# Routed attention and an ELU feed-forward: row sums inverted on 32 partitions by way of transfers, weights converted within attention, one form of the second product for all groups

## The chip, the cores and the metric

The kernel runs on one core of a Trainium2 chip. The engines of the core are TensorE (PE, matrix products; PEld is its weight load), VectorE (DVE), ScalarE (ACT), GpSimd (POOL) and SyncE (SP, which here issues transfers, DMAs). The metric is the device time in microseconds of one execution, as the median of several runs.

## The reference

Attention runs over 4 batches, 8 heads, 768 tokens, head size 64. Each query and each key is assigned to one of 16 centroids of its head, and a query sees only the keys of its own cluster:

```python
    mask = q_assign[:, :, :, None] == k_assign[:, :, None, :]
    scores = scale * np.matmul(q, k.transpose(0, 1, 3, 2))
    scores = np.where(mask, scores, -1000000000.0)
    scores = scores - np.max(scores, axis=-1, keepdims=True)
    attn = np.exp(scores)
    attn = attn / (np.sum(attn, axis=-1, keepdims=True) + 1e-09)
    return np.matmul(attn, v).astype(np.float32)
```

Its output, 3072 tokens of 512 values, goes through `h = x @ w_in` (512 to 2048), an ELU, and `g @ w_out` (2048 to 512). The two weights arrive as 64-bit floats, all else is worked in 32 bits.

## The kernel before

**Attention.** There are 32 blocks: batch, half of the queries (384), pair of heads. `slot(n)` is one step of a software pipeline. PE's work in it, in order: the row sums of block n-2 (`row_sums`, L551, a product with ones that spreads each sum over 64 partitions), the products with V of block n-1 (`values`, L533), in some slots a product with the centroids (`similar`, L424), and the scores of block n (L495, with a mask product at L508). ACT takes the exponentials of block n (L517). DVE adds the probabilities over the keys (`sums_begin` L520, `sums_end` L525 and L526), so that the sums of block n are begun at the end of slot n and ended at the start of slot n+1. The division of block n-2 in slot n works on all 128 partitions: ACT takes the logarithm of the sums, a copy of them, and the exponential of minus the logarithm (`take_sums`, L560 to L562); DVE makes one Newton step (`divide`, L565 and L566) and POOL multiplies the block's output with it (L569).

Also in the slots, on DVE: the cluster assignment (L437 to L450), the transposes of the next batch's raw keys and queries (L652 to L666), and the conversion of the 64-bit weights. On SP, in program order within a slot: `load_v(n + 1)` (L179), `load_k` and `load_q` (L163: a `load_k` is 4 transfers, a `load_q` 16), then the 1 MB pieces of 64-bit weights (`ask`, L297). `load_q` comes in slots 1 and 4 of a batch (2 and 4 of the first), `load_k` twice in slot 0 and once in slots 2 and 3. SP issues in order, and an issue that must wait for an engine or for another transfer holds back what comes after it.

**Conversion.** 16 pieces, eight of `w_in`, eight of `w_out`. A piece is fetched to a place (`places`), then a "begin" (L317, L325, and on ACT L327) and three "join" steps (L337, L341, L347) on DVE. `weigh(n)` doles them out: slot n adds ROOM[n] us to a credit, and a step is taken while the credit covers its COST. Four sums of quarters of `w_out` follow (`weight_sum`, L372 to L378). What is left after attention is done at the `fill()` points of group 0.

**Feed-forward.** 3072 tokens in 6 groups of 512. The first product of a group is four units (`unit`, L735) of seven block products each, by a scheme of the Strassen kind, with the additions on DVE and ACT. In a unit, L788 adds product 5 into bank 2 before the block product `block_product(b2, s4, x22, False)`; the ELU is ACT's exponential (L745), a clamp on POOL (L746) and L749 on DVE. A unit has four `fill()` points. In group 0 POOL also makes the sums of `w_in` (`w_step`, L714 to L718) and sends them to DRAM (`w_far`, L719), and later groups fetch them from there (L711).

The second product has seven units of the same scheme over quarters of `w_out`. In groups 1 to 5 each of them is again seven small products (`second_product`, L919, with DVE's `t_step` L962 to L968 and `g_step` L979), 49 in all, of four 128 by 128 products each. For that 33 tables of sums and quarters of `w_out` are made by `table_steps` (28 steps on DVE, L876 to L883, sent to DRAM by L869), two steps at each `fill()` of group 1, and read back part by part (`fetch`, L914). In group 0, `second_product_plain` makes each unit from eight small products per quarter pair, 56 in all, without tables. `verdict` puts the findings of `findings` into a flag that decides whether a general path must run; it doesn't here.

Of the kernel before, what the change touches and what calls it, by code (L numbers as in the profile page):

```python
# [19 lines left out]
P = 128  # L20
# [41 lines left out]
def main_path(ctx, tc, c, q, k, v, centroids, moe_w_in, moe_w_out, out):  # L62
# [77 lines left out]
    r_of = sums_w[:, 6 * HS : 7 * HS]  # L140
    e_of = sums_w[:, 7 * HS : 8 * HS]
# [109 lines left out]
    r_sum = const.tile([P, len(blocks)], F32, name="r_sum")  # L251
    d_sum = const.tile([P, len(blocks)], F32, name="d_sum")
# [21 lines left out]
    places += [(spare.rearrange("p a n -> p (a n)")[:, : 2 * WC].unsqueeze(1), into + 2)]  # L274
# [78 lines left out]
    def by_chunks(x):  # L353
# [9 lines left out]
        "s2": by_chunks(t_all),  # L363
        "s4": by_chunks(sums_w[:, 1536:3584]),
        "s3": by_chunks(words_w[:, :]),
    }

    def weight_sum(n):
# [13 lines left out]
        [0.0, 1.0, 1.3, 1.4, 1.4, 1.7, 2.6, 2.6]  # L382
        + [2.3, 2.6, 3.0, 3.0, 1.4, 1.7, 2.6, 2.6] * (B - 2)
        + [2.3, 2.6, 4.0, 4.0, 2.6, 2.6, 2.6, 2.6]
    )
    COST = {"begin": 1.4, "join": 1.25, "sum": 2.2}
# [11 lines left out]
    def weigh(n):  # L398
        nonlocal credit, now
        now = n  # L400
        credit = min(credit, 2.5) + ROOM[n]
        begun = False
        while steps and credit >= COST[steps[0][0]]:
            kind, m = steps[0]
            if kind == "join" and begun or kind == "sum":
                return
            if kind == "begin" and asked_in.get(m, n) > n - 2:
                return
            credit -= COST[kind]
            begun = begun or kind == "begin"  # L410
            weigh_step(*steps.pop(0))
# [134 lines left out]
    def take_values(n):  # L546
        nc.scalar.activation(x_of(n), o_bank[:, :HS], Act.Copy, scale=-1.0)
# [11 lines left out]
    def take_sums(n):  # L559
        nc.scalar.activation(r_of, d_bank[:, :HS], Act.Ln)  # L560
        nc.scalar.activation(e_of, d_bank[:, :HS], Act.Copy, accum_out=d_sum[:, n : n + 1])
        nc.scalar.activation(r_of, r_of, Act.Exp, scale=-1.0)  # L562

    def divide(n):
        nc.vector.tensor_tensor(e_of, e_of, r_of, op=Alu.mult)  # L565
        nc.vector.scalar_tensor_tensor(  # L566
            r_of, e_of, -2.0, r_of, op0=Alu.add, op1=Alu.mult, accum_out=r_sum[:, n : n + 1]
        )
        nc.gpsimd.tensor_tensor(x_of(n), x_of(n), r_of, op=Alu.mult)  # L569
# [55 lines left out]
    def slot(n):  # L625
# [16 lines left out]
        if n > 1:  # L642
            divide(n - 2)
# [24 lines left out]
        weigh(n)  # L668

# [91 lines left out]
    def unit(k_, u, after_second=None, fill=None):  # L761
# [20 lines left out]
        if k_ == 1 and u == 3:  # L782
# [15 lines left out]
        if k_ > 0:  # L798
            for t in {2: ("t1",), 3: ("t2", "t3", "t4")}.get(u, ()):
                t_step(0, t)  # L800
# [61 lines left out]
    def table_steps():  # L862
# [9 lines left out]
        for n, a in enumerate(("s3", "s4", "s2", "a11", "a12", "s1", "a22")):  # L872
# [21 lines left out]
    for n in range(len(UNITS)):  # L894
# [9 lines left out]
        for _ in range(1, N // GS)  # L904
# [122 lines left out]
    def second_product_plain(k_, early_on):  # L1027

        for n in range(len(UNITS)):
            _, a, b = UNITS[n]  # L1030
            for q_ in range(4):
                for j in range(2):
                    small_product(
                        banks_of(k_, n)[q_],
                        part_g(b, j, q_ % 2),
                        part_w(a, q_ // 2, j),
                        j == 0,
                        j == 1,
                    )
                if n == 0 and q_ == 0:  # L1040
                    flush_all()
                    early_on()
                elif n == 2 and q_ == 1:
                    verdict()
                take(k_, n, q_)
            taken(k_, n)
            if n < 3:
                g_step(n, 0)
                g_step(n, 1)
            if n == 2:  # L1050
                next_group(k_)

    def second_product(k_, ahead):
# [17 lines left out]
        for n in range(len(UNITS)):  # L1071
            b1, b2, b3, b4 = (x[:, :P] for x in banks_of(k_, n))
            part_product(k_, n, "m6")
            nc.scalar.copy(b3, b2)
            if n > 0:
# [34 lines left out]
    def findings():  # L1110
# [3 lines left out]
        nc.vector.tensor_reduce(peak[:, 0:1], r_sum, axis=Axis.X, op=Alu.add)  # L1114
        nc.vector.tensor_reduce(peak[:, 1:2], d_sum, axis=Axis.X, op=Alu.add)
        nc.vector.tensor_scalar(ok[:, 0:1], peak[:, 0:1], -R_MAX, None, op0=Alu.is_gt)
        nc.vector.tensor_scalar(ok[:, 1:2], peak[:, 1:2], D_MAX, None, op0=Alu.is_lt)
# [13 lines left out]
    for n in range(1, len(blocks)):  # L1131
        slot(n)
        if n == 3 * NB + 1:
            places.append((early[:, 6144:].unsqueeze(1), into + 6))
            ask()
# [8 lines left out]
    row_sums(last_n - 1)  # L1144
    values(last_n)
    sums_end()
    for n in range(2):
        places.append((p_out[:, ts(n, 2048)].unsqueeze(1), len(pieces)))
    ask()
    take_sums(last_n - 1)  # L1150
    divide(last_n - 1)
    take_values(last_n)

    def finish_attention():
        row_sums(last_n)
        take_sums(last_n)
        divide(last_n)
# [9 lines left out]

    def fill_weights():
        flush()
        if steps:  # L1170
            weigh_step(*steps.pop(0))

    def early_on():
        while steps:
            weigh_step(*steps.pop(0))
            flush()

    blanks(0)
    for u in range(4):
        if u == 1:  # L1180
            blanks(1)
        run(unit(0, u, finish_attention if u == 0 else None, fill_weights))
        if u == 1:
            findings()
    second_product_plain(0, early_on)

    table = table_steps()

    def fill_table():
# [274 lines left out]
```

## Time and profile before

| what | value |
| --- | --- |
| median of 3 runs | 915.13 us (914.92 to 915.49) |
| the profiled execution | 915.41 us, span 913.5 us from first to last instruction |
| attention | to 341.4 us |
| group 0, four units | 341.4 to 393.8 us |
| group 0, second product | 393.8 to 444.1 us |
| group 1, four units | 444.1 to 492.5 us |
| group 1, second product | 492.5 to 536.4 us |

The page gives one line for each engine with its busy time, then the span in 40 slices with the busy tenths. A view of windows gives, for each stretch, the busy time and number of instructions of PE, PEld, DVE, ACT and POOL, then the clock granted to PE, the share of the DMA engines and GB/s. In a timeline a line is start, duration, engine, source line, operation, out<-in, shape and count, with idle time of the engine before it and who ended it in brackets. A view of one source line gives minimum, median and maximum of its durations in ns, and for transfers the time from issue to landing.

### The profile page before, as it was taken

To read this page: it belongs to the slowest core of one execution; us is meant where nothing else is said; L and a number is where in the kernel's file an instruction comes from. 1 tells how busy PE (TensorE), PEld (TensorE's weight loads), DVE (VectorE), ACT (ScalarE), POOL (GpSimd) and SP (SyncE) were. 2 spreads that over 40 slices of the span, in tenths; PEclk is the share of its full clock that TensorE was granted. 3 is DMA by queue.
4 is the path that set the end of the run, shared out by engine and by line. 5 is a ranking of instruction groups with operands and counts; after the bars stand their busy time and mean duration, and the time that the engine had idled before them with its cause. 6 is when DMAs were issued, how large, how long until landed. Compare 5 with 4: busy or idle time off the path is not lost.

```text
span 913.5 us, 15842 instructions
## 1 busy us (share of the span) xinstructions
PE 898.5 (98%) x6083; PEld 685.4 (75%) x6083; DVE 673.8 (74%) x980; ACT 416.9 (46%) x819; POOL 201.5 (22%) x197
## 2 busy tenths in 40 slices
PE   7999999999999999999999999999999999999996
PEld 5444444444444448899988998999899989998996
DVE  4799999999999996982389843684369446944584
ACT  5767787777778764410133223322332233223321
POOL 1022121131304326750025002400230013102200
PEclk9999999999999999999999999999999999999999
DMA  6755554354325431110297852185218521762172
GB/s 201 190 107 150 139 137 104 103 110 128 68 83 137 146 110 69 52 42 2 87 319 263 285 170 66 45 280 173 70 37 278 182 69 36 266 196 61 45 224 81
DMA packets 143331, 121.22 MB, mean 133 GB/s; under 512 B 88208, under 2 KB 104592, under 8 KB 142224
## 3 DMA queue, kind: packets, MB, share of 16 engines
q1 hardware_dynamic: 142000, 115.93, 43.2%
q0 software_dynamic: 1248, 4.20, 1.5%
q8 instruction: 50, 0.82, 0.4%
q14 instruction: 33, 0.27, 0.1%
HBM read 100.96 MB, written 18.09 MB: 130 GB/s over the span
## 4 chain that ended last, share of the span: by engine, by line
PE 88%; DVE 7%; POOL 2%; issue 1%; DMA 1%; ACT 1%; DVEq 0%; SPq 0%; POOLq 0%; ACTq 0%
PE bank L919 23%; PE bank L735 22%; PE banks L495 12%; PE o_bank L533 11%; PE o_bank L735 4%; PE o_bank L919 4%; PE banks L508 3%; PE d_bank L551 2%; PE d_bank L919 2%; PE d_bank L735 2%; PE d_bank L424 1%; PE banks L574 1%; DVE sums_w L525 1%; DVE sums_w L520 1%; DVE sums_w L526 1%
## 5 line engine op out<-in xcount | busy, mean ns | idle before, releaser
L517 ACT ACTIVATE p_out<-banks 128x768 f32<-128x768 f32 x192 | 155.2, 812 | 26.8 <-PE banks L508 25.4
L746 POOL TENSOR_SCALAR kq_g<-kq_g 128x512 f32<-128x512 f32 x96 | 71.5, 753 | 389.9 <-ACT kq_g L745 389.6
L533 PE MATMUL o_bank<-p_out,kq_g 128*64 128x384 f32 x768 | 129.4, 486 | 0.3 <-DMA kq_g<-in_v_dram 0.3
L533 PEld LDWEIGHTS o_bank<-p_out,kq_g 128*64 128x64 f32 x768 | 55.0, 137 | 69.4 <-issue 62.7
L749 DVE SCALAR_TENSOR_TENSOR kq_g<-kq_g,bank 128x512 f32<-128x512 f32 x72 | 48.3, 684 | 67.0 <-POOL kq_g L746 67.0
L735 PE MATMUL bank<-xT,w_in 128*128 128x256 f32 x384 | 90.7, 379 | 0.0
L569 POOL TENSOR_TENSOR xT<-xT,sums_w 128x384 f32<-128x384 f32 x32 | 35.4, 1105 | 222.0 <-DVE sums_w L566 147.0
L735 PEld LDWEIGHTS bank<-xT,w_in 128*128 128x128 f32 x384 | 72.6, 190 | 10.1
L735 PE MATMUL bank<-x_sum,w_in 128*128 128x256 f32 x288 | 68.0, 379 | 0.0
L735 PE MATMUL bank<-xT,spare 128*128 128x256 f32 x288 | 66.3, 379 | 0.7 <-DVE bank L788 0.7
L919 PE MATMUL bank<-w_out,kq_g 128*128 128x128 f32 x512 | 62.9, 275 | 0.0
L520 DVE TENSOR_TENSOR sums_w<-p_out 128x1536 f32<-128x1536 f32 x32 | 57.1, 1785 | 7.6 <-ACT p_out L517 7.6
L525 DVE TENSOR_TENSOR sums_w<-sums_w,p_out 128x1536 f32<-128x1536 f32 x32 | 59.0, 1845 | 3.3 <-DVE sums_w L520 0.5
L735 PEld LDWEIGHTS bank<-xT,spare 128*128 128x128 f32 x288 | 54.6, 190 | 8.4 <-issue 1.0
L919 PEld LDWEIGHTS bank<-w_out,kq_g 128*128 128x128 f32 x512 | 60.4, 192 | 0.3
L735 PEld LDWEIGHTS bank<-x_sum,w_in 128*128 128x128 f32 x288 | 54.6, 190 | 7.3
L745 ACT ACTIVATE kq_g<-bank 128x512 f32<-128x512 f32 x72 | 42.0, 597 | 39.0 <-PE bank L735 37.4
L979 DVE TENSOR_TENSOR kq_g<-kq_g 128x1024 f32<-128x1024 f32 x36 | 45.0, 1257 | 2.7 <-PE bank L919 2.7
L460 POOL TENSOR_SCALAR kq_g<-w_out,big,minus 128x768 bf16<-128x768 bf16 x16 | 33.9, 2124 | 47.3 <-ACT w_out L453 47.3
L495 PE MATMUL banks<-x_sum,xT 64*128 64x384 f32 x192 | 39.8, 492 | 0.0
L495 PE MATMUL banks<-kq_g,xT 64*128 64x384 f32 x192 | 39.6, 491 | 0.0
L495 PE MATMUL banks<-kq_g 64*128 64x384 f32 x192 | 39.6, 491 | 0.0
(238 smaller groups left out, 1708.1 us busy)
## 6 DMA issues: line engine op xcount, KB each, us to landing
spare<-w_far SPq DMA_DIRECT2D x60, 256.0 KB, 2.7
kq_g<-in_v_dram SPq DMA_DIRECT2D x32, 384.0 KB, 3.6
sums_w<-far_s_s SPq DMA_DIRECT2D x40, 256.0 KB, 3.9
words_w<-far_s_s SPq DMA_DIRECT2D x29, 256.0 KB, 3.6
out_dram<-p_out SPq DMA_DIRECT2D x24, 256.0 KB, 2.6
w_out<-in_q_dram SPq DMA_DIRECT2D x112, 48.0 KB, 2.5
words_w<-far_a_s SPq DMA_DIRECT2D x21, 256.0 KB, 3.4
sums_w<-far_s_q SPq DMA_DIRECT2D x21, 256.0 KB, 3.1
```

Source lines behind the costliest of these rows:

```text
L495: nc.tensor.matmul(s[:, e, :HS], lhsT=kT[b % 2][pr][rows, ts(kt, P)], rhs=qT[half][pr][rows], start=True, stop=False,)
L517: nc.scalar.activation(probs[kt], s[:, :, :HS], Act.Exp, scale=SCALE)
L520: nc.vector.tensor_tensor(add_to, probs_all[:, : 4 * HS], probs_all[:, 4 * HS : 8 * HS], op=Alu.add)
L525: nc.vector.tensor_tensor(add_to, add_to, probs_all[:, 8 * HS :], op=Alu.add)
L533: nc.tensor.matmul(o_bank[64 * e : 64 * e + 64, :HS], lhsT=v_raw[n % 2][:, e, kt], rhs=probs[kt][:, e], start=(kt == 0), stop=(kt == NT - 1),)
L569: nc.gpsimd.tensor_tensor(x_of(n), x_of(n), r_of, op=Alu.mult)
L735: nc.tensor.matmul(bank[:, ts(f, QS)], lhsT=left[:, ch, ts(f, P)], rhs=right[:, ch], start=first and f == 0 and ch == 0, stop=ch == 1, ski ...
L745: nc.scalar.activation(to, bank.rearrange("p (f n) -> p f n", f=2), Act.Exp)
L746: nc.gpsimd.tensor_scalar(to, to, 1.0, 0.0, op0=Alu.min, op1=Alu.max)
L749: nc.vector.scalar_tensor_tensor(to, to, -1.0, bank.rearrange("p (f n) -> p f n", f=2), op0=Alu.add, op1=Alu.max)
L919: nc.tensor.matmul(bank[:, :P], lhsT=left[:, f], rhs=right[:, f], start=first and f == 0, stop=last and f == 3, skip_group_check=True,)
L979: nc.vector.tensor_tensor(b[to][:, f], b[x][:, f], b[y][:, f], op=op)
```

## The change

- `take_sums(n)` makes one copy of the sums (ACT) and issues, on SP, two transfers that lay row 0 and row 64 of it, 384 sums each, over 32 partitions (12 a partition). `invert(n)` makes the reciprocals there and a reduction for the findings (DVE). `spread(n)` issues three transfers on SP: the reciprocals to a buffer in DRAM (`far_r`), and from there each head's row to 64 partitions. `divide(n)` is POOL's multiplication alone. In slot n come `take_sums(n - 2)`, `divide(n - 4)`, `invert(n - 3)` and, after `weigh(n)`, `spread(n - 3)`. The last three blocks are finished in units 0 to 2 of group 0.
- ROOM grows by 0.8 in most slots; `weigh` may also take the first two sums of `w_out`; FROM keeps the pieces of `w_out` that lie over attention's raw keys and queries until these are done. The fetched pieces lie in two places until piece 15, and the late places are gone.
- In group 0 the fills take the other two sums and then three table steps each; `second_product` serves group 0 as well, and `second_product_plain` is gone. The fetches of the tables start in unit 3 of group 0. The findings come in unit 2.

The core of the diff:

```diff
-    r_of = sums_w[:, 6 * HS : 7 * HS]
-    e_of = sums_w[:, 7 * HS : 8 * HS]
+    r_places = [sums_w[:, 6 * HS : 7 * HS], kq_g[:, 7168 : 7168 + HS]]
+    e_of = [sums_w[:, 7 * HS : 8 * HS], spare.rearrange("p a n -> p (a n)")[:, 2560 : 2560 + HS]]
...
-    places += [(spare.rearrange("p a n -> p (a n)")[:, : 2 * WC].unsqueeze(1), into + 2)]
+    places += [(spare.rearrange("p a n -> p (a n)")[:, : 2 * WC].unsqueeze(1), into + 7)]
...
-        [0.0, 1.0, 1.3, 1.4, 1.4, 1.7, 2.6, 2.6]
-        + [2.3, 2.6, 3.0, 3.0, 1.4, 1.7, 2.6, 2.6] * (B - 2)
-        + [2.3, 2.6, 4.0, 4.0, 2.6, 2.6, 2.6, 2.6]
+        [0.0, 1.0, 1.3, 2.2, 2.2, 2.5, 3.4, 3.4]
+        + [3.1, 3.4, 3.8, 3.8, 2.2, 2.5, 3.4, 3.4] * (B - 2)
+        + [3.1, 3.4, 4.8, 4.4, 4.0, 4.0, 4.0, 4.6]
     )
+
+    FROM = {3: 21, 4: 24, 5: 24, 6: 25, 7: 26}
...
-            if kind == "join" and begun or kind == "sum":
+            if kind == "join" and begun or kind == "sum" and m > 1:
                 return
-            if kind == "begin" and asked_in.get(m, n) > n - 2:
+            if kind == "begin" and (asked_in.get(m, n) > n - 2 or n < FROM.get(m - into, 0)):
...
     def take_sums(n):
-        nc.scalar.activation(r_of, d_bank[:, :HS], Act.Ln)
-        nc.scalar.activation(e_of, d_bank[:, :HS], Act.Copy, accum_out=d_sum[:, n : n + 1])
-        nc.scalar.activation(r_of, r_of, Act.Exp, scale=-1.0)
+
+        e = e_of[n % 2]
+        nc.scalar.copy(e, d_bank[:, :HS])
+        for h in range(2):
+            nc.sync.dma_start(
+                inverse[n % 2][:few, 0, h],
+                e[64 * h : 64 * h + 1].rearrange("o (p j) -> o p j", p=few),
+            )
...
+    def invert(n):
+        both = inverse[n % 2][:few]
+        nc.vector.reciprocal(both[:, 1], both[:, 0])
+        nc.vector.tensor_reduce(
+            peaks[:few, n], both.rearrange("p x h j -> p x (h j)"), axis=Axis.X, op=Alu.add
+        )
+
+    def spread(n):
+
+        nc.sync.dma_start(
+            far_r[n % 2].rearrange("h (p j) -> p h j", p=few), inverse[n % 2][:few, 1]
+        )
+        for h in range(2):
+            nc.sync.dma_start(
+                r_of(n)[64 * h : 64 * h + 64], far_r[n % 2][h : h + 1].to_broadcast([64, HS])
+            )
 
     def divide(n):
-        nc.vector.tensor_tensor(e_of, e_of, r_of, op=Alu.mult)
-        nc.vector.scalar_tensor_tensor(
-            r_of, e_of, -2.0, r_of, op0=Alu.add, op1=Alu.mult, accum_out=r_sum[:, n : n + 1]
-        )
-        nc.gpsimd.tensor_tensor(x_of(n), x_of(n), r_of, op=Alu.mult)
+        nc.gpsimd.tensor_tensor(x_of(n), x_of(n), r_of(n), op=Alu.mult)
...
-        if n > 1:
-            divide(n - 2)
+        if n > 3:
+            divide(n - 4)
+        if n > 2:
+            invert(n - 3)
...
         weigh(n)
+        if n > 2:
+            spread(n - 3)
...
-    def finish_attention():
-        row_sums(last_n)
-        take_sums(last_n)
-        divide(last_n)
+    def finish_attention(u):
+        if u == 0:
+            row_sums(last_n)
+            take_sums(last_n)
+            divide(last_n - 2)
+            invert(last_n - 1)
+            spread(last_n - 1)
+        elif u == 1:
+            divide(last_n - 1)
+            invert(last_n)
+            spread(last_n)
+        elif u == 2:
+            divide(last_n)
+            findings()
...
     def fill_weights():
         flush()
         if steps:
             weigh_step(*steps.pop(0))
-
-    def early_on():
-        while steps:
-            weigh_step(*steps.pop(0))
-            flush()
...
+        else:
+            for _ in range(3):
+                next(table, None)
+
     for u in range(4):
...
-    second_product_plain(0, early_on)
...
-    for k_ in range(1, N // GS):
...
+    for k_ in range(N // GS):
+        if k_:
+            for u in range(4):
+                run(ahead if u == 0 else unit(k_, u))
         ahead = unit(k_ + 1, 0) if k_ + 1 < N // GS else iter(())
         second_product(k_, ahead)
```

## The prediction

> **What bounds the kernel now.** I read the page's engine table and slices first. TensorE (PE) is busy 98% of a 913.5 us span at nearly full clock, so time changes only where PE's work changes or where PE is made to wait.
>
> ```profile
> span 913.5 us, 15842 instructions
> ...
> PE 898.5 (98%) x6083; PEld 685.4 (75%) x6083; DVE 673.8 (74%) x980; ACT 416.9 (46%) x819; POOL 201.5 (22%) x197
> ...
> PE   7999999999999999999999999999999999999996
> ...
> DVE  4799999999999996982389843684369446944584
> ...
> PEclk9999999999999999999999999999999999999999
> ```
>
> DVE (VectorE) is as full as PE in the first sixteen slices. So the second view was the busy time of each engine by stage (us, then PE, PEld, DVE, ACT, POOL): the stages are one batch of attention (slots 8 to 15), the four units of group 0, its second product, the units of group 1, its second product.
>
> ```profile
> 105.38:186.20 80.82, 80.82 (x546) 37.48 (x544) 78.25 (x92) 60.95 (x100) 17.00 (x12) 1.00 0.53 132
> 341.40:393.80 52.40, 50.97 (x235) 42.95 (x234) 43.90 (x54) 21.38 (x38) 33.66 (x34) 1.00 0.21 75
> 393.80:444.10 50.30, 50.30 (x452) 50.13 (x451) 22.16 (x34) 3.99 (x14) 11.83 (x6) 1.00 0.05 19
> 444.10:492.50 48.40, 48.40 (x227) 42.29 (x225) 37.48 (x54) 17.16 (x31) 10.55 (x14) 1.00 0.81 262
> 492.50:536.40 43.90, 43.35 (x379) 42.92 (x378) 37.59 (x70) 10.49 (x41) 8.41 (x7) 1.00 0.72 232
> ```
>
> Attention slots take 9.71 us, or 10.49 with a cluster product (timeline of PE); PE waits in them only 0.5 us in slot 3 and 0.9 in slot 23. Slot n starts with the row sums of block n-2. Third view, the queue of SP (SyncE), which issues nearly all transfers:
>
> ```profile
> 214.70 3.26 SPq L163 DMA_DIRECT2D w_out<-in_k_dram  x4
> 220.90 0.37 SPq L179 DMA_DIRECT2D kq_g<-in_v_dram  x1
> 226.65 11.50 SPq L163 DMA_DIRECT2D w_out<-in_q_dram  x16
> ```
>
> One load_q holds SP for a whole slot: 16 issues, 0.67 us apart. SP's own part in attention is no wait of PE yet.
>
> **The change, part by part.** The sum goes against the profiled execution: 915.41 us, 1.9 of them outside its span of 913.5; the median of the three runs, 915.13, is 0.3 lower.
>
> *Second product of group 0.* 7x4x2x4 = 224 small products become 49x4 = 196. 393.8 to 444.1 becomes a stage like 492.5 to 536.4: 50.3 against 43.35 busy. By count 28 x 0.2235 us (80 records, two a product, in 8.93 us on the chain) = **-6.25**. The blanks of group 1 go (-0.4), and its 0.55 wait at 498.8 may go as the tables leave it: together **-0.9**.
>
> *Units of group 0.* DVE is the limit there already: PE waits twice for DVE's L788 addition (bank 2 += product 5), 0.66 us each. The timeline shows the first (start, duration, instruction):
>
> ```profile
> 363.97 0.68 DVE L788 TENSOR_TENSOR o_bank<-o_bank,spare 128x512 f32<-128x512 f32 x1
> ...
> 364.80 0.45 PE L735 MATMUL o_bank<-xT,spare 128*128 128x256 f32 x1 [0.66 <-DVE o_bank L788]
> ```
>
> From L788 of unit 0 (348.83) to that of unit 3 (389.39), DVE spends 40.6 us: 3.7 idle, 21.4 on conversions, the first weight sum and the findings, so 15.4 on the units themselves. After the change it has 15.4, two weight sums (2.2+2.6), inversions 0.6, findings 0.8, one t1 0.65 and all 28 table steps before unit 3's L788, as ten fills of three come by then. A step takes 0.61 to 0.72 alone and up to 1.13 beside POOL; in group 1 the 28 took 22.1, 3.6 over 28x0.66. So 22.3 + 28x0.66 = 40.7, plus c, what POOL adds: at least 2.6 (group 1's 3.6 less a quarter for unit 3, though POOL is busy 10.6 us there and 33.7 here), at most 9 (0.5 for each of 18 meetings); I take 6, nearer to this stage's own rows (L325 takes 2.06 at 374.37, 0.69 elsewhere). Waits on POOL's clamp add 0.8 (0 to the 2.7 of unit 0 now). DVE then needs 47.5 from the first L788 to the fourth; PE's three periods are 3x12.07 (seven products of 1.725) + 0.4 = 36.6, and unit 0 leaves 2.6 in hand. PE waits 8.3, against 1.6 now: **+6.7**, from +2.5 to +11.6. Unit 3 has no fills left, so nothing spills into the second product. Groups 0 and 1 together: -6.25-0.9+6.7 = **-0.45** (-4.7 to +4.5).
>
> The Trainium skill ("SBUF — State Buffer", two separate sides) says that a DVE operation with two SBUF inputs and a GpSimd operation exclude each other for a whole instruction. Rows of group 1 agree in kind (L876 1.10 against 0.68) but cost 0.2 us per POOL operation; the full rule, some 19 us of POOL work in three units, would by an estimate make these units about 13 us slower still.
>
> *Conversions.* Counted through the planner's credits, all 16 pieces end by slot 29 and two sums stand in slot 30; before, 13 pieces and a begin by slot 31. DVE in attention gains 2.75 pieces (about 4.9 each) and 4.6 to 5.7 of sums, +19, and loses the two divisions' operations, 1.04 a slot, for two on 32 partitions, about 0.3 (L239's reciprocal 0.16 and L1119's reduction 0.17 are rows of one to 16 elements; bounds 0.2 to 0.6): -23. Nothing by itself; PE covers it. ACT loses 1.2 us a slot (0.48+0.20+0.52); it is not the limit.
>
> *The way of the sums.* This sets my forecast. Each slot adds five transfers to SP: two rows to 32 partitions, one to DRAM, two broadcasts that must wait, on SP, until the DRAM write has landed, since they read it. What is queued behind: load_v, load_k, load_q, weight pieces and the next slot's rows, and DVE's inversion stands in order ahead of transposes, conversions and the next sums. The nearest rows: an issue of 0.32 to 0.37 us (L914, L179) and 0.05 to the next, landing 2.0 after issue at least (stores of L1015).
>
> ```profile
> L914 SPq DMA_DIRECT2D sums_w<-far_s_s x40: 319/320/797, 485.3 to 884.2; - x40
> ...
> DMA to landing us min/median/max: 2.0/2.6/3.5
> ...
> DMA to landing us min/median/max: 4.8/5.5/11.9
> ```
>
> The second line is that of the stores, the third that of the weight pieces (L297). Transfers land in order: behind such a piece the q loads of 20.0 to 22.4 us all land near 31. SP's time over slots 8 to 15: two load_q 21.3, 16 load_k 10.7, eight load_v 3.4, four pieces 1.7 = 37; new 40 issues x0.42 = 16.8, eight waits of 1.6 = 12.8, and in slots 9, 10, 12, 14 the write goes behind a piece, 3.4 more each = 13.6. Together **80 of PE's 80.8**. SP can't choose its moments (load_q of slot 12 waits for DVE's transpose), so it falls behind.
>
> I carried four clocks through the slots: PE's rows; DVE's own time per slot in the trace, less 1.04 and the old steps, plus 0.3 and the new steps; the copy on ACT; SP as above. A slot's rows must land before DVE's inversion in the next slot. PE waits when DVE is over 5.8 us behind (row sums) or over 3.7 where a begin precedes a cluster product, as in slot 23. The same sums for the kernel before end attention's last slot at 336.6; the trace has 336.7. After: SP leaves slots 9, 10 and 11 15 to 17 us late, with load_q, a load_k and two pieces. It starts on slot 12 at 149.7: rows 150.5, load_v, load_q to 161.6, the piece 162.0, the write lands 167.0, broadcasts 167.9, slot 13's rows land 170.3. DVE is at that inversion, in slot 14, at 165.2 and waits 5.1. In all DVE waits 1.5 us in slot 6, 3.8 in 11 and 12, 5.1 in 14, 4.5 in 22, 5.9 in 28 (there behind the accumulating transfer that made a load_v take 11 us). Of these 20.8 PE sees **13.9**, 10.2 of them in slots 12 to 15; the waits of before, 1.4, go: **+12.5**. With 0.3 an issue it is 5.8, with landing 0.3 sooner 8.7 and 0.6 sooner 4.7, both 1.1; with 0.62 an issue (rows behind q) 29.
>
> The Trainium skill ("DMA: Bandwidth & Descriptors", two DMAs through the same engine) asks the issuing engine to wait for the first transfer's completion before one that reads it; the trace has SP waiting so once, for w_far. The same page's fixed cost of about 2.0 us a transfer agrees with the stores; its word that a sequencer's issue time is usually small would have made the SP sum nothing and the forecast 915.
>
> After attention the last three blocks are needed only by the last group, so their waits cost nothing unless POOL's clamp stands behind a division: that is in the 2.7 above.
>
> **Forecast**: 915.1+12.5-0.45 = **927**; own range 920 to 936; chance 0.50.
>
> **Rivals.** (1) *SP keeps up*: small transfers issue in 0.3 and land in 1.4, rows always precede the inversion, and PE waits in attention for nothing. Then -1.4 there and -4.7 to 0 in the groups: 909 to 913.7, taken as 912, **faster**, 0.20. For it: SP is idle for whole slots in 21 to 24 and the rows have a slot of slack; against: 11.50 us for a load_q. It decides where SP's backlog stays under about 12 us in slots 12 and 20. (2) *SP is worse*: its small issues cost 0.62 as in the rows behind load_q, or writes land later among packets under 512 B (88208 of 143331): 29 of PE wait, 943; 936 to 955, 0.17. (3) *SP keeps up, but table steps meet POOL harder*, or the tables' buffers wait for their writes (33 of 256 KB in some 35 us is 247 GB/s, near group 1's 262): 913.3 to 920; 0.13, of which 0.08 within 0.2%. That the change doesn't save its 28 products I exclude.
>
> Measurement of this kernel tells 0.2% from no change. Faster 0.20, same 0.08, slower 0.50+0.17+0.05 = 0.72. The range leaves out the upper half of rival 2 and the best of rival 1: 911 to 946.
>
> **What would show it.** Right: SP's waits for a transfer into far_r stand high, DVE idle before the L-line of the reciprocal with a DMA as releaser, slots of 12 to 15 us around slots 12 to 15 and 22, 43.9 for group 0's second product, 58 to 60 for its units. Wrong: attention slots still at 9.71 and 10.49 and DVE never idle at the reciprocal.

## The result and the profile after

| | before | after |
| --- | --- | --- |
| median | 915.13 us (4 runs, 914.92 to 915.49) | 963.1 us (4 runs, 958.27 to 963.7) |
| ratio | | 1.0511 (95% interval 1.0497 to 1.0526) |
| profiled execution | 915.41, span 913.5 | 963.7, span 961.9 |
| attention ends | 341.4 | 384.9 (+43.5) |
| group 0, four units | 52.4 | 64.9 (+12.5) |
| start of group 0's second product to start of group 1's | 99.5 | 92.5 (-7.0) |

The rest of the span differs by -0.6 us, so the rows add up to 48.4. The change makes the kernel 5.1% slower. The prediction had the sign right, but 927, its range of 911 to 946 included, is far too low.

The page of the kernel after, with the same lines as were shown of before (busy time of each engine, then the span in 40 slices):

```profile
span 961.9 us, 16152 instructions
...
PE 907.5 (94%) x6021; PEld 684.3 (71%) x6023; DVE 681.1 (71%) x989; ACT 389.5 (40%) x751; POOL 192.6 (20%) x198
...
PE   7997997789969999969999999999999999999997
...
DVE  4786995699859999799844684478348734963584
...
PEclk9998998989989999989999999999999999999999
```

Two things are new. PE and DVE have holes in the same slices (4, 7, 8, 12), which suggests that both wait for a third party; the timelines below name it. (In slice 18, the units of group 0, DVE is full, and PE waits for it.) And PEclk, all nines before, has eights in or just after the holes. The view of windows over attention (length, then busy time of PE, PEld, DVE, ACT and POOL, the granted clock, DMA share, GB/s) separates the two effects. Before:

```profile
0.00:341.40 341.40, 335.35 (x2318) 160.18 (x2319) 312.75 (x375) 251.93 (x408) 77.22 (x61) 1.00 0.49 127
```

After, attention and the four units of group 0:

```profile
0.00:384.90 384.90, 348.40 (x2317) 163.18 (x2317) 315.82 (x358) 221.12 (x317) 73.88 (x60) 0.96 0.50 130
...
384.90:449.80 64.90, 54.17 (x232) 45.57 (x233) 54.59 (x71) 18.48 (x33) 34.27 (x37) 0.92 0.60 197
```

In attention PE's idle time grows from 6.05 (341.40 less 335.35) to 36.5, by 30.4; and the same 2,300 products take 13.1 more **busy** time, at a mean clock of 0.96. In the units idle time grows from 1.4 to 10.7 and busy time from 50.97 to 54.17. So of the 48.4 us, 39.7 are waits, 16.3 are the same products run slower, and 7.6 come off elsewhere. By the clock's record PE works 21.1 us of attention at half clock, which accounts for 10.6 of the 13.1; the other 2.5 are not traced.

One place in slots 6 and 7 shows the whole chain. The queue of SP:

```profile
72.74 10.64 SPq L163 DMA_DIRECT2D w_out<-in_q_dram  x16
83.42 0.61 SPq L586 DMA_DIRECT2D far_r<-inverse  x1
87.15 1.13 SPq L590 DMA_DIRECT2D sums_w<-far_r  x2
88.38 1.21 SPq L569 DMA_DIRECT2D inverse<-spare  x2
```

SP is held for 10.64 us by `load_q`, then sends one block's reciprocals to DRAM (83.42), stands still until they have landed (the gap to 87.15), issues the broadcasts, and only then the rows of the next block (88.38). DVE meanwhile, in the bracket its idle time and who ended it:

```profile
82.83 0.96 DVE L531 TENSOR_TENSOR sums_w<-sums_w 128x768 f32<-128x768 f32 x1
90.79 0.29 DVE L579 RECIPROCAL inverse<-inverse 32x24 f32<-32x24 f32 x1 [7.00 <-DMA inverse<-spare]
91.12 0.19 DVE L580 TENSOR_REDUCE peaks<-inverse 32x2 f32<-32x48 f32 x1
91.24 0.56 DVE L442 STREAM_TRANSPOSE w_out<-d_bank 128x384 f32<-128x384 f32 x1
```

A reciprocal of 0.29 us waits 7.00 for those rows, and behind it in DVE's order stands L442, which frees the bank that PE's row sums need:

```profile
85.11 0.33 PE L513 MATMUL banks<-kq_g,w_out 64*128 64x384 bf16 x2
91.85 1.55 PE L556 MATMUL d_bank<-sums_w,ones 128*64 128x384 f32 x4 [6.42 <-DVE w_out L442]
93.18 4.28 PE L538 MATMUL o_bank<-p_out,kq_g 128*64 128x384 f32 x20
```

The four row sums then take 1.55 us; the same four take 0.87 at full clock (`split_new`, 165.82). The windows around the pause tell why (the clock is the third number from the end):

```profile
82.00:88.10 6.10, 3.44 (x28) 1.70 (x24) 1.69 (x2) 4.23 (x6) 0.00 (x0) 1.00 0.22 36
88.10:95.00 6.90, 3.15 (x10) 1.12 (x12) 4.07 (x9) 1.02 (x2) 3.28 (x3) 0.51 0.70 238
```

PE's pause of 6.42 us begins at 85.4; from 88.1, still within it, until 95.0 PE is granted half its clock. The same follows the other long pauses. The stretches at half clock last 3.4, 6.8 or 10.2 us, 30.7 in attention and 10.2 in the units.

The sums over all blocks, from the waits (total, times, longest), first SP's queue, then DVE:

```profile
SPq L590 <- DMA far_r<-inverse: 104.0, 32, 8.2
```

```profile
DVE inverse L579 <- DMA inverse<-spare: 28.0, 4, 8.9
...
DVE inverse L579 <- DMA inverse<-sums_w: 9.6, 4, 4.3
```

SP stands 3.25 us a block (104.0 over 32) for its own write to land; DVE waits 37.6 us for rows, in eight blocks only. SP can't make this up: from the row issues of slot 8 to those of slot 16,

```profile
113.99 1.22 SPq L569 DMA_DIRECT2D inverse<-sums_w  x2
...
209.54 1.17 SPq L569 DMA_DIRECT2D inverse<-sums_w  x2
```

it needs 95.6 us, without another idle stretch than 28.7 for landing and one of 0.4, where PE needs 80.8 for eight slots.

### The profile page after: what moved, and what is told of

The parts are those of the page before. It is cut to its first block, busy times and chain, and to the rows that moved or that the text cites. A ratio compares the mean times of both kernels' runs of the same rounds, so it can differ in the third digit from the quotient of the medians.

```text
span 961.9 us, 16152 instructions
## 1 busy us (share of the span) xinstructions
PE 907.5 (94%) x6021; PEld 684.3 (71%) x6023; DVE 681.1 (71%) x989; ACT 389.5 (40%) x751; POOL 192.6 (20%) x198
## 4 chain that ended last, share of the span: by engine, by line
PE 78%; DVE 10%; DMA 5%; SPq 4%; issue 2%; ACT 1%; POOL 0%; DVEq 0%; ACTq 0%; POOLq 0%
PE bank L765 22%; PE bank L949 21%; PE o_bank L538 8%; PE banks L500 8%; PE o_bank L765 4%; PE o_bank L949 4%; SPq L163 3%; DMA far_r<-inverse 3%; PE banks L513 2%; PE d_bank L765 2%; PE d_bank L949 2%; PE d_bank L556 2%; PE banks L600 1%; DVE sums_w L525 1%; DVE sums_w L530 1%
## 5 line engine op out<-in xcount | busy, mean ns | idle before, releaser
L776 POOL TENSOR_SCALAR kq_g<-kq_g 128x512 f32<-128x512 f32 x96 | 67.5, 711 | 402.1 <-ACT kq_g L775 402.0
L538 PE MATMUL o_bank<-p_out,kq_g 128*64 128x384 f32 x768 | 136.3, 507 | 5.6 <-DMA kq_g<-in_v_dram 5.6
L595 POOL TENSOR_TENSOR xT<-xT,sums_w 128x384 f32<-128x384 f32 x29 | 37.6, 1295 | 245.6 <-DMA sums_w<-far_r 234.1
L530 DVE TENSOR_TENSOR sums_w<-sums_w,p_out 128x1536 f32<-128x1536 f32 x32 | 63.3, 1977 | 2.9
L949 PE MATMUL bank<-w_out,kq_g 128*128 128x128 f32 x384 | 48.7, 275 | 0.0
L556 PE MATMUL d_bank<-sums_w,ones 128*64 128x384 f32 x128 | 29.8, 545 | 20.1 <-DVE w_out L442 18.8
L949 PE MATMUL bank<-sums_w,p_out 128*128 128x128 f32 x376 | 48.3, 275 | 0.0
L998 DVE TENSOR_TENSOR p_out<-kq_g,p_out 128x512 f32<-128x512 f32 x42 | 34.5, 821 | 17.4 <-PE bank L949 16.9
L949 PEld LDWEIGHTS bank<-w_out,kq_g 128*128 128x128 f32 x384 | 46.2, 192 | 0.3
L949 PEld LDWEIGHTS bank<-sums_w,p_out 128*128 128x128 f32 x376 | 45.3, 192 | 0.1
L552 ACT COPY xT<-o_bank 128x384 f32<-128x384 f32 x32 | 15.3, 479 | 71.1 <-PE o_bank L538 71.1
```

What stands on the lines that cost most here:

```text
L530: nc.vector.tensor_tensor(add_to, add_to, probs_all[:, 8 * HS :], op=Alu.add)
L538: nc.tensor.matmul(o_bank[64 * e : 64 * e + 64, :HS], lhsT=v_raw[n % 2][:, e, kt], rhs=probs[kt][:, e], start=(kt == 0), stop=(kt == NT - 1),)
L556: nc.tensor.matmul(d_bank[64 * e : 64 * e + 64, :HS], lhsT=ones, rhs=summed[:, ts(e, HS)], start=True, stop=True,)
L595: nc.gpsimd.tensor_tensor(x_of(n), x_of(n), r_of(n), op=Alu.mult)
L776: nc.gpsimd.tensor_scalar(to, to, 1.0, 0.0, op0=Alu.min, op1=Alu.max)
L949: nc.tensor.matmul(bank[:, :P], lhsT=left[:, f], rhs=right[:, f], start=first and f == 0, stop=last and f == 3, skip_group_check=True,)
```

## The experiments

Each kernel ran once, beside one run of the kernel before on the same chip: 915.32 for the first four (`sums_alone`, `old_sums`, `pool_queue`, `no_landing_wait`), 914.9 for `split_old`, `split_new`, `blanks_in_pauses` and `no_pool_sums`, 915.22 for `pe_pauses` and `rows_on_96`, 916.0 for `begin_later` and `two_steps_a_fill`. The kernel after varied by 5 us over its four runs, so differences of less are read from the stages of the traces. "Excess" below is the time of the attention slots (2 to 30) over 9.71 us, or 10.49 with a cluster product; the kernel after has 43.4.

**The two halves of the change.** `sums_alone` is the kernel before with the new `take_sums`, `invert`, `spread` and `divide`. `old_sums` is the kernel after with

```diff
-        e = e_of[n % 2]
-        nc.scalar.copy(e, d_bank[:, :HS])
...
+        nc.scalar.activation(r_of, d_bank[:, :HS], Act.Ln)
+        nc.scalar.activation(e_of, d_bank[:, :HS], Act.Copy, accum_out=d_sum[:, n : n + 1])
+        nc.scalar.activation(r_of, r_of, Act.Exp, scale=-1.0)
```

and the division of before.

> Only the way of the row sums is taken over into the kernel before; the planner, the places and group 0 stay as before (13 pieces in attention, the plain second product). Theory (the five transfers a slot hold up SyncE, rows land after VectorE needs them, TensorE waits and its clock falls): attention still ends 20 to 45 us later than 341.4, about 935 to 960 us in all. Rival (the conversions moved into attention overload VectorE): attention ends within 3 us of 341.4, total 912 to 918.

> The changed kernel with the old division (logarithm, exponential, Newton step on 128 partitions) and everything else as changed: all conversions in attention, tables in group 0, 49 products. Theory: SyncE's backlog is gone, so no long waits in slots 12 to 15 and 22 to 23; VectorE has about 0.7 us a slot more than in the changed kernel, for which the running sum gives 11 us of waits; with the 5 us of group 0 about 925 to 935. Rival (conversions in attention): still 950 or more.

Measured: `sums_alone` 943.74 (+28.4), attention to 367.3, excess 27; SP waits 98.3 us for far_r. `old_sums` 932.81 (+17.5), attention to 357.3, excess 15.2, units 62.6 us. The two add up to 45.9 of 48: nearly independent. The way of the sums is the larger half, but the rest, which I had put at about nothing, costs 17.5 (15.9 in attention, 10.2 in the units, less the second product's gain).

**What in the way of the sums costs: the issues, or the wait for the landing?** `pool_queue` issues the five transfers from GpSimd (`nc.sync` becomes `nc.gpsimd` in `take_sums` and `spread`). `no_landing_wait` keeps all issues on SP, but

```diff
-                r_of(n)[64 * h : 64 * h + 64], far_r[n % 2][h : h + 1].to_broadcast([64, HS])
+                r_of(n)[64 * h : 64 * h + 64], far_r[(n + 1) % 2][h : h + 1].to_broadcast([64, HS])
```

so that a broadcast reads what landed a slot before (the output is divided by another block's sums).

> The changed kernel with the five transfers of the sums issued by GpSimd, whose queue has little else to do in attention. Theory: SyncE is as free as before, VectorE waits for rows at most once or twice, attention ends within 6 us of 341.4; group 0 stays 5 us longer: 915 to 928. Rival (the transfers themselves, their number or landing time, are too slow for one slot of slack): VectorE still waits 20 us or more, 945 to 965.

> The two broadcasts read the reciprocals of the block before, already in DRAM, instead of this block's, so the outputs are divided by other sums; number and size of transfers stay, but SyncE needn't wait for this block's write to land. It splits the backlog: of SyncE's time for the sums, 104 us are waits for landing and about 32 x 5 x 0.63 = 100 us are issues. Theory (time on SyncE's queue, whichever kind): attention's excess falls from 43 to 5 to 20 us, total 920 to 945. Rival (issue alone decides, landing waits lie beside idle time): 955 or more. Rival (landing waits alone): as without any backlog, under 922.

Measured: `no_landing_wait` 928.34, excess 9.4 instead of 43.4, no wait for a write into far_r: **one wait on SP is worth 34.8 us** of 48 (963.1 less 928.34; 34.0 of them in the attention slots), with as many transfers as in the kernel after. `pool_queue` 942.44, between its theory and its rival: attention ends at 353.6, but the units take 75.7 us, since POOL's clamp, which DVE needs for the ELU, now stands behind transfers that wait (DVE waits 14.8 us for the clamp there, 1.7 in the kernel after):

```profile
353.60:429.30 75.70, 56.48 (x232) 46.67 (x233) 54.12 (x71) 18.32 (x33) 40.59 (x52) 0.89 0.52 172
```

The cost moved to another queue.

**The same without changing what is computed.** `split_old` (the kernel before with the way of the sums) and `split_new` (the whole change) issue the broadcasts one slot after the transfer to DRAM:

```diff
+        if n > 3:
+            widen(n - 4)
         if n > 2:
             spread(n - 3)
```

where `widen` is the loop of two broadcasts out of `spread`; `divide` comes a slot later as well.

> The kernel before with the new way of the sums only (as in sums_alone), but the two broadcasts of a block are issued one slot after its transfer to DRAM, and its division one slot later. The output stays the reference's. Theory (SP's standing wait for its own transfer into DRAM is what costs, not the number of transfers): SP waits for that landing no more, DVE's inversions find their rows, attention ends within 3 us of the 341.4 of before (sums_alone 367.3), PE's clock is never halved there, total 912 to 918. Rival (the five issues of about 0.6 us are enough to put SP behind): excess over the usual slot lengths of 10 us or more, 925 or more.

> The whole change with the same edit: broadcasts one slot after the transfer to DRAM, division one slot later. The output stays the reference's. Theory: the landing wait goes as in no_landing_wait, attention's excess over the usual slot lengths falls from 43.4 to 8 to 12 us, and what is left stands in the slots that the larger ROOM fills with conversions (10, 15, 22, 29, 30), not at the inversions; total 924 to 932. Rival (the conversions cost nothing, the residue of no_landing_wait came from the transfers): excess under 4, total under 921.

Measured: `split_old` 919.59 (above its expected 918), excess 0.06, attention to 341.0; the wait that was 98.3 us is down to

```profile
SPq L590 <- DMA far_r<-inverse: 15.0, 8, 3.9
```

None of its transfers is gone. Five issues a block are therefore no burden for SP; the standing wait was. (The broadcasts now also wait for POOL's division to have read the buffer that they overwrite, 11.4 us in attention, which costs nothing there.) What remains, 4.7 us, lies in the units (56.7 instead of 52.4), where the last blocks are finished. On DVE's timeline:

```profile
382.10 0.69 DVE L781 SCALAR_TENSOR_TENSOR kq_g<-kq_g,bank 128x512 f32<-128x512 f32 x1 [5.07 <-POOL kq_g L778]
```

DVE waits 5.07 us for POOL's clamp. Ahead of the clamp POOL has the last division, which starts at 378.32 after waiting 3.45 us for its broadcasts; this edit issues those only when the division before them has read the one buffer that both use. PE then pauses for 1.5 and 2.3 us. `split_new` 934.21, excess 10.4: above its expected 932, and the residue is as in `no_landing_wait`; as `split_old` has none, it belongs to the conversions. Its units take 69.9 us, 5.0 more than in the kernel after; there too POOL's last division waits for its broadcasts (6.1 us) and DVE for the clamp behind it (4.6).

**What of the conversions costs.** In `split_new` 6.1 of the 10.4 us stand in slot 15. DVE, then ACT, then PE:

```profile
172.83 0.68 DVE L328 TENSOR_SCALAR sums_w<-w_out 128x1024 uint32<-128x1024 uint32 x1
```

```profile
173.55 1.15 ACT L330 ACTIVATE sums_w<-sums_w,off 128x1024 uint32<-128x1024 uint32 x1 [4.48 <-DVE sums_w L328]
174.60 0.46 ACT L567 COPY spare<-d_bank 128x384 f32<-128x384 f32 x1
```

```profile
175.11 1.50 PE L429 MATMUL d_bank<-xT,cT 128*32 128x384 f32 x8 [4.55 <-ACT spare L567]
```

Slot 14 has three joins and then a begin. The begin's part on ACT waits 4.48 us for DVE's, ACT's copy of the sums stands behind it, and PE's cluster product of slot 15 needs the bank that this copy frees. `begin_later` is `split_new` with that one begin moved by a slot:

```diff
-            if kind == "begin" and (asked_in.get(m, n) > n - 2 or n < FROM.get(m - into, 0)):
+            if kind == "begin" and (asked_in.get(m, n) > n - 2 or n < FROM.get(m - into, 0) or n == 14):
```

> split_new with one conversion step moved: the begin of piece 7, which stands at the end of slot 14 behind three joins, comes at slot 15 instead; all pieces are still converted by slot 29. The output stays the reference's. Theory (the residue of the conversions is this: ACT's half of a begin waits for DVE's at the end of a full slot, ACT's copy of the sums stands behind it, and PE's cluster product of slot 15 needs the bank that the copy frees): the excess of 6.1 us in slot 15 goes, the half-clock stretch after it too, attention ends near 345, total 926 to 930. Rival (DVE is simply over its time per slot, wherever the step stands): the excess moves to slots 16 and 17 and the total stays within 2 us of 934.

Measured: 931.63, excess 8.4. Slot 15 falls from 6.1 to 0.95, as the theory has it, but slot 17 rises from 0 to 3.9, as the rival has it. Both are partly right: the planner now puts three joins and a begin into slot 16, again ahead of a cluster product. The same four steps in slots 9, 19, 25 and 28, where no cluster product follows, cost at most 0.8 us (the slot after 25) in either kernel. So the place decides, as well as the amount; a planner that keeps a begin out of full slots ahead of a cluster product wasn't tried.

**The units of group 0.** On the kernel after, a table step beside POOL (DVE, then POOL in the same microseconds):

```profile
404.29 3.22 DVE L913 TENSOR_TENSOR sums_w<-words_w,sums_w 128x512 f32<-128x512 f32 x1
...
408.56 2.22 DVE L908 TENSOR_TENSOR sums_w<-sums_w 128x512 f32<-128x512 f32 x1
```

```profile
404.12 0.58 POOL L749 DMA_DIRECT2D w_far<-spare  x1 [0.30 <-POOL spare L748]
404.72 1.01 POOL L595 TENSOR_TENSOR xT<-xT,kq_g 128x384 f32<-128x384 f32 x1
405.67 1.28 POOL L744 TENSOR_TENSOR spare<-w_in 128x512 f32<-128x512 f32 x1
```

The step of 3.22 us ends after the last of the three POOL instructions. `no_pool_sums` takes POOL's sums out of units 1 to 3:

```diff
-        if n == 0:
+        if u > 0:
+            pass
+        elif n == 0:
             nc.gpsimd.tensor_tensor(s2, s1, a11, op=Alu.subtract)
```

> The whole change, but in units 1 to 3 of group 0 POOL does not make its three sums of w_in for each unit (their transfers stay, and send what lies there), so this kernel leaves out that part of the computation. Theory (POOL's sums are what makes DVE's table steps long in these units): table steps L906 to L913 take 0.61 to 0.75 nearly throughout, where they took up to 3.2 beside POOL; DVE's four additions at L819 span 42 to 46 us instead of 52.0, and the units take 54 to 58 us instead of 64.9; total 953 to 957, with attention as in the kernel after. Rival (the units are long for DVE's own work, or for waits of the tables' buffers): the table steps shorten little, the span stays over 49 and the total over 960.

Measured: 958.25, attention as after (to 384.3), units 60.4 instead of 64.9, somewhat above the 54 to 58 expected. The 28 table steps take 21.5 us together instead of 30.0; none is over 1.4. So POOL's sums are the reason for the long steps, 8.5 us of DVE time. But PE gains only half of it: its first wait falls from 4.9 to 0.6 us, the second stays (6.3 after 5.7), because another wait comes up, this kernel's list of what DVE waits for at its L908 (the after's L906):

```profile
  DMA far_s_s<-p_out: 2.3, 1
  DMA far_s_s<-sums_w: 1.8, 1
  DMA far_a_s<-p_out: 1.7, 1
```

With shorter steps DVE comes sooner to buffers whose writes to DRAM aren't done: 5.8 us, where the kernel after has 1.2. `two_steps_a_fill` asks whether it is the bursts or the total, on top of `begin_later`:

```diff
-            for _ in range(3):
+            for _ in range(2):
                 next(table, None)
```

> begin_later, with two table steps at each fill of group 0 in place of three (what is left by unit 3 is made there at once, ahead of the fetches). The output stays the reference's. Theory (the units wait for DVE since the bursts of three steps fall on POOL's sums ahead of the additions PE needs; total DVE work, some 55 us, is above PE's 48 in any case): PE's waits in units 1 and 2 fall, the wait ahead of the last additions grows, the units take 60 to 66 us where split_new took 69.5, total 920 to 926. Rival (only the total of DVE's work in the units counts): units within 2 us of those of begin_later.

Measured: 934.39, the units 70.3 us against 69.3: the rival. PE's first wait falls from 4.9 to 2.2, the last one grows from 5.3 to 10.7. That fits DVE's work in this stage, 54 to 55 us, most of which has to be done before the last additions, whatever its order.

**PE's clock.** `blanks_in_pauses` fills three of the pauses with products of the blank tile:

```diff
+        if n in (7, 15, 23):
+            free = pair_tiles[(turn_of + 1) % 3]
+            for m in range(24):
+                nc.tensor.matmul(
...
```

> The whole change, with 24 products of the blank tile (512 columns, about 5.2 us at full clock) put on PE ahead of the row sums of slots 7, 15 and 23, the places where PE pauses for 6.4, 4.9 and 7.1 us waiting for DVE. They compute nothing that is used. Theory (a pause is followed by a stretch at half clock, which costs half its length again): the half-clock stretches after those places go, some 20 us of them, and the time falls by 5 to 10 us though PE does 15 us more work: 953 to 958. Rival (the half clock has another cause, or costs nothing since DVE and SP are late anyway): the half-clock stretches stay, or go without effect, and the time is 963 or more.

Measured: 960.82, between theory and rival. The half-clock time in attention falls from 30.7 to 10.2 us, attention ends 3.7 us sooner (381.2), the total is within the spread of the four runs of after. So the stretches do come from the pauses, but removing 20 us of them gives back 3.7 at most, not 10; and 1.8 of the 3.7 stand in slots 12 and 13, where no blank product was put. A likely reason, which no run shows by itself: after a pause PE is not the only one that is late, and where DVE or SP still is, a faster PE waits. `pe_pauses` measures the clock by itself, in the kernel before, where nothing else is late (m = 1, 5, 10, 20 in groups 2 to 5):

```diff
+    def pause(k_, m):
+        bank = sets[k_ % 2][1]
+        every = blank[:, 0:1].to_broadcast([P, 512])
+        nc.tensor.matmul(bank, lhsT=blank, rhs=every, start=True, stop=True)
+        for _ in range(m):
+            nc.scalar.copy(junk, bank[:, :P])
+        nc.tensor.matmul(bank, lhsT=junk, rhs=every, start=True, stop=True)
```

> The kernel before, with one pause of PE put into each of groups 2 to 5, ahead of unit 2, where nothing else makes PE wait: PE waits for a chain of 1, 5, 10 or 20 small copies on ACT that start from one of its own products. The output stays the reference's. Theory (a pause costs its own length and, from some length on, half of a stretch at half clock that follows it): gaps of about 0.8, 1.8, 3 and 6 us; the granted clock stays at 1.0 after the first, and is 0.5 for 3.4 to 7 us after the last two; the time grows by the sum of the gaps (11 to 14 us) and by 4 to 7 us more, 929 to 936. Rival (the half clock in the kernel after has another cause than PE's pauses, such as the transfers or the conversions beside them): no half-clock stretch, and the time grows by the gaps alone, 925 to 929.

Measured: 931.94 (+16.7). PE's timeline at the four pauses; the line after a pause is the first block product, 8 records:

```profile
561.99 0.39 PE L728 MATMUL bank<-blank,junk 128*128 128x512 bf16 x1 [0.36 <-ACT junk L727]
562.21 1.89 PE L744 MATMUL bank<-xT,w_in 128*128 128x256 f32 x8
...
656.26 0.39 PE L728 MATMUL o_bank<-blank,junk 128*128 128x512 bf16 x1 [1.54 <-ACT junk L727]
656.48 1.89 PE L744 MATMUL bank<-xT,w_in 128*128 128x256 f32 x8
...
752.01 0.61 PE L728 MATMUL bank<-blank,junk 128*128 128x512 bf16 x1 [3.03 <-ACT junk L727]
752.41 3.12 PE L744 MATMUL bank<-xT,w_in 128*128 128x256 f32 x8
...
852.13 0.61 PE L728 MATMUL o_bank<-blank,junk 128*128 128x512 bf16 x1 [5.99 <-ACT junk L727]
852.53 3.62 PE L744 MATMUL bank<-xT,w_in 128*128 128x256 f32 x8
```

After 0.36 and 1.54 us of idle time the block product takes 1.89 as always; after 3.03 and 5.99 it takes 3.12 and 3.62. The clock in the windows that follow:

```profile
752.01:755.40 3.39, 3.39 (x10) 2.75 (x11) 0.00 (x0) 0.00 (x0) 0.00 (x0) 0.58 0.00 0
...
852.13:857.30 5.17, 5.17 (x13) 4.09 (x14) 0.00 (x0) 1.06 (x2) 0.00 (x0) 0.50 0.00 0
857.30:860.70 3.40, 3.40 (x17) 3.00 (x16) 0.69 (x1) 0.99 (x3) 0.61 (x1) 1.00 0.00 0
```

From one group's second product to the next's is 92.9, 92.1, 92.1 and 92.1 us in the kernel before, and 93.9, 94.3, 97.2 and 101.2 here: +1.0, +2.2, +5.0, +9.1. Less the gap and two products of the blank tile (0.22 each) that leaves 0.2, 0.2, **1.6 and 2.7** for half-clock stretches of 0, 0, 3.4 and 6.8 us. Both stretches begin before the pause ends; PE works 2.9 and 5.2 us in them, half of which is 1.4 and 2.6. That confirms the theory, for the part of a stretch in which PE works.

**What an issue costs.** `rows_on_96` lays the sums over 96 partitions (`few = 96`).

> The whole change with the sums laid over 96 partitions (4 a partition) in place of 32 (12 a partition): the same number of transfers and bytes, in three times as many pieces. The output stays the reference's. Theory A (SP's issue time of these transfers, 0.58 us against 0.32 for the kernel's large ones, goes with the number of pieces): row issues (L569) of 0.9 us or more, SP further behind, the time 972 to 995. Theory B (0.5 to 0.6 us is what an issue costs in this queue whatever its pieces): row issues 0.55 to 0.62 as before, the time within 5 us of 963.

Measured: 963.93, and the row issues (min/median/max in ns), first of the kernel after:

```profile
L569 SPq DMA_DIRECT2D inverse<-sums_w x32: 538/584/600, 41.5 to 383.7; - x32
```

then with three times as many pieces:

```profile
L569 SPq DMA_DIRECT2D inverse<-sums_w x32: 538/588/854, 40.3 to 384.3; - x32
```

Theory B: the number of pieces doesn't set the issue time (a few issues take longer, up to 1.2 us).

No version beats the kernel before; the nearest is `split_old` at +4.7 us.

## Why the prediction was right or wrong

**Second product of group 0: right.** -6.25 and -0.9 were predicted, -7.0 measured; group 1's wait of 0.55 is gone.

**The way of the sums: right mechanism, far too small.** What the prediction said would show it is there: SP's waits into far_r, DVE idle at the reciprocal, long slots at 12 to 15 and 22. Attention was to lose 12.5 us and lost 43.5. The step that failed is SP's time over slots 8 to 15, "80 of PE's 80.8": it was 95.6, so SP was not just full but 15 us short in this batch, and a term was missing besides.

- *"new 40 issues x0.42"*: the row issues take 0.584 and stand 0.62 apart, the broadcasts take 0.51, only the writes 0.43. In these slots the 40 took some 24 us instead of 16.8, and the loads, put at 37, some 43. I had taken the issue of a large fetch (L914) as the nearest row; the rows behind `load_q`, 0.67 apart, were nearer. This is the condition of rival 2, and its 29 us of PE waits are close to the 30.4 of added idle time.
- *"eight waits of 1.6"*, plus 3.4 more in four slots: that is 26.4 us in eight slots, and 28.7 were measured. This size was right. But with the issues and loads too cheap SP seemed able to keep up between its late slots, and so the waits came out too short: slot 6 cost 6.7 us where DVE was to wait 1.5 and PE for less, slots 12 to 15 20.4 instead of 10.2, slots 22 and 23 12.0; slot 28's predicted wait didn't come.
- *Missing: PE's clock.* The prediction let a wait cost its own length. The same products take 13.1 us more busy time in attention and 3.2 in the units. How much of the 13.1 is lost for good stays open, as `blanks_in_pauses` gave back at most 3.7 for two thirds of the half-clock time. The page showed a clock of nines throughout, and the kernel before has no pause of a whole microsecond in attention, so its trace alone couldn't price this. The Trainium skill could have ("TensorE: Matmul & The Clock Gate", Part 1): PE falls to half its clock after an idle window of about 3.4 us. The stretches here, 3.4 and 6.8 us, fit that window; its threshold doesn't, since PE need not be idle for the whole of it: 3.03 us was enough in `pe_pauses`, and 2.10 in `begin_later` (191.8) were followed by 3.4 us at half clock.

**Conversions: wrong.** "Nothing by itself; PE covers it" was a sum over whole slots, with DVE's balance of +19 and -23. With no wait for the landing, 8 to 10 us stay in attention (`no_landing_wait`, `split_new`, `begin_later`). The prediction itself had the rule that applies ("over 3.7 where a begin precedes a cluster product") and didn't carry it into the slots that the larger ROOM fills. In `old_sums`, where the old division stays on DVE, it is 15.2.

**Units of group 0: right mechanism, at the upper end and a little over.** +6.7 was predicted, +2.5 to +11.6 allowed, +12.5 measured. DVE's four additions span 52.0 us (47.5 predicted). The term that was mis-sized is c, what POOL adds: I took 6, the 28 steps took 30.0 for 18.5 (28x0.66), so 11.5, above my bound of 9; `no_pool_sums` shows 8.5 of it to be POOL's sums. The other term is the clock again, 3.2 us of busy time. On the Trainium skill's rule of mutual exclusion ("SBUF — State Buffer", two separate sides): steps of 2.2 and 3.2 us that outlast POOL instructions speak for it here, where the rows of group 1, 1.10 at most, hid it. The true cost lies between the rows' price, which I took, and the rule's.

**The chances.** The likeliest case and rival 2 were kept apart as if only SP's issue time decided. In truth the bad ends came together: a late SP makes PE pause, and a pause costs clock; no case had both, and with units at their upper end too the sum was outside the range.

## What to carry to other kernels

A transfer that reads what another has just written should be issued a stage later, not behind a wait in the same queue: the same transfers cost 28.4 us with the wait and 4.7 without it (`sums_alone`, `split_old`). A PE that is 98% busy has a second price for waits: a pause of some 2 us or more can be followed by 3.4 to 10.2 us at half clock, so price waits by length and number, not by their sum alone; where other engines are late as well, less of that price is real. Add up the queue that issues the transfers as carefully as an engine, every issue and every wait at the price of the nearest rows in the same queue. Compare a stage's balance not only in total but at the instruction that frees the bank PE needs next: a conversion step that is free in one slot cost 4 to 6 us in another.

## What the runs showed of the hardware

- PE's granted clock after a pause: full after 0.36 and 1.54 us, half for 3.4 us after 3.03, half for 6.8 after 5.99 (`pe_pauses`). Pauses near 2 us go either way: 2.10 (`begin_later`) was followed by 3.4 us at half clock, 2.38 in `old_sums` (347.6) by none.
- What decides is where the pause falls. In each trace the edges of the half-clock stretches lie whole multiples of 3.41 us apart, as on a fixed grid. Counted over the 13 traces with such stretches, from 30 us on: of the cells of that grid that had full clock and in which PE was idle for 1.97 us or more, all 49 were followed by a cell at half clock; of those with 1.77 us or less, none of 3244; the eight between went either way. Of the 2.10 us, 2.04 lie in one cell; an edge at 348.3 cuts the 2.38 into 0.7 and 1.7. After a half-clock cell with 0.73 us of idle time or more the next had half clock too, with 0.59 or less it had full clock.
- The issue of a row of 384 sums on SP takes 0.584 us (median) laid over 32 partitions and 0.588 over 96.
- A DVE instruction of 0.68 us with two SBUF inputs took 2.2 and 3.2 us beside two or three consecutive POOL instructions.
